# A decode layer with streamed K and V: the products of V are moved inside a loop trip, and the spreading of the heads is moved behind the loop

## The chip, the cores and the metric

The kernel runs on one core of a Trainium2 chip. The metric is the device time of one execution in microseconds (us). It was measured three times before the change: 297.23, 297.03 and 293.18 us, median 297.03 us. A profiled execution of the same program, from which all rows below come, took 297.05 us; the span of its instructions is 295.7 us.

## The reference

One decode step of a transformer layer for two sequences (B = 2, one new token each), in bf16:

```python
x  = A_x                                            # 2 x 1 x 640
q  = layernorm(x) @ wq                              # 32 heads of 192
k  = k_cache[:, :, 8192 - 2048:, :]                 # 2 x 32 x 2048 x 192, the last 2048 positions
v  = v_cache[:, :, 8192 - 2048:, :]
p  = softmax(q @ k.T * 192 ** -0.5)                 # per batch and head
h  = x + (p @ v, heads side by side) @ wo           # wo: 6144 x 640
h2 = h + (gelu(layernorm(h) @ w_gate) * (layernorm(h) @ w_up)) @ w_down   # 640 -> 1536 -> 640
```

K and V of the window are 50 MB each; the weights are some 22 MB. Each byte is read once and used for one or two vectors.

## The kernel before

**Tiles.** The window of a batch is cut into four quarters of 512 positions. One quarter of K, or of V, for all 32 heads is one transfer of 6144 KB into a 48 KB slot of each partition (`load_k`, `load_v`). A partition holds 128 positions of one head; 32 heads by four pieces make 128 partitions. A quarter is worked on as two groups of 64 positions per partition. So there are 16 groups g in all, 8 per batch; quarter g // 2 of K and of V belongs to group g.

**One group.** `transposes(g)` (line 560) turns the group's K on TensorE in 12 chunks of four matmuls, each chunk into one of four PSUM banks (`tps[0]` to `tps[3]`, used in turn); seven chunks are copied out to `ktr` by VectorE and five by ScalarE (lines 571 and 569). `scores(g)` (line 618) multiplies `ktr` with the masked queries into the bank `sps`. `softmax(g)` (lines 628 to 633) takes minimum and exponentials; `e_turn(g)` (line 657) and `e_blocks(g)` (line 661) put the exponentials, transposed, into the buffer `eblk[g % 2]`. `pv(g)` (line 673) multiplies them with V: 64 matmuls into the bank `ops` for even g and into `m1` for odd g.

**One trip.** TensorE and VectorE run a hardware loop of four trips J over groups 4J to 4J+3, that is two quarters, half a batch. After the trip's four groups `maxima`, `sums` and `combine` (lines 637 to 693) make the softmax's correction factors `wp` and `wfin`. The first quarter's products are copied from PSUM to `osb` (line 683). The second quarter's products, `pv(4J+2)` and `pv(4J+3)`, stand in `behind`, which runs at the start of the next trip (segment "pa", left out in trip 0) or behind the loop; `behind` also adds all four groups' products, weighted, into `osum` (lines 696 to 705).

**The heads.** After a batch, `heads_done(b)` scales `osum` into `onrm` and spreads it: four fp32 matmuls with the selection matrix `colsel` (line 714) into two PSUM banks, and for each bank a masked product, a reduction and a copy on VectorE (lines 720 to 724), which give `ot`, the stationary operand of the output projection. Batch 0's call stands in trip 2, in a segment of its own ("op", emitted under a condition on the trip); batch 1's stands behind the loop, ahead of the output projection `oproj` (line 738), the second layernorm and the feed-forward part (lines 806 to 889).

**What sets the order.** Each engine runs its instructions in the order in which the calls below are written; there is no planner. Between engines there are semaphores, derived from the reads and writes that each operation names. All large transfers are issued by SyncE in one fixed order: wq, k0, k1, v0, k2, v1, k3, v2, and so on to v7, then the four pieces of wo, w_gate, w_up and w_down. A transfer is issued when the last TensorE operation that reads the old content of its place is done (`done`, `pump`). The ring has three slots: two for K, one for V (v7 goes into a K slot). So v(i+1) is issued when `pv` of the odd group of quarter i is done, k(i+2) when the transposes of the odd group of quarter i are done, wo's first three pieces when `pv(13)` is done, wo's last piece, w_gate and w_up after `transposes(15)`, and w_down after `pv(15)`.

Of the kernel before, what the change touches and what calls it, by code (L numbers as in the profile page):

```python
# [6 lines left out]
F32 = mybir.dt.float32  # L7
# [5 lines left out]
B = 2  # L13
# [233 lines left out]
def bass_sequential_preLN__sliding_block_cached__geglu_ffn__decode_kernel(  # L247
# [12 lines left out]
    with ExitStack() as ctx:  # L260

        def sb(name, shape, dt):
            return ctx.enter_context(nc.sbuf_tensor(name, shape, dt))
# [64 lines left out]
        eblk = sb("eblk", [128, 2, 16, 4, 32], BF16)  # L328
        osb = sb("osb", [128, 2, DH], F32)
        osum = sb("osum", [128, DH], F32)  # L330
        onrm = sb("onrm", [128, DH], F32)
        cti = sm[:, 0:384].bitcast(I32).rearrange("p (k x) -> p k x", k=3)
        cxi = ktr[:, 0, :].bitcast(I32)[:, 0:512]
        cxf = ktr[:, 1, :].bitcast(F32)[:, 0:512]
# [80 lines left out]
        def dve(fn, R=(), W=(), X=(), cls=1):  # L415
            return P.op("dve", fn, R, W, X, cls=cls if looped else 0)
# [4 lines left out]
        def pe(fn, R=(), W=(), X=(), cls=0):  # L421
            return P.op("pe", fn, R, W, X, cls=cls)
# [4 lines left out]
        def ts(out, in0, s1, op0, s2=None, op1=None):  # L427
            def fn(e):
                kw_ = {"op1": op1} if op1 is not None else {}
                return e.tensor_scalar(out=out, in0=in0, scalar1=s1, scalar2=s2, op0=op0, **kw_)  # L430
            return fn
# [117 lines left out]
        def transposes(g, lo, hi):  # L549

            kk, ktoks = where["k", g // 2]
            kv = kk.bitcast(F32)
            for n in range(lo, hi):
                c, ch, scalar = TR[n]
                bank, x = tps[n % 4], ("t", n % 4)

                def fn(e, c=c, ch=ch, bank=bank):
                    for u in range(4):
                        off = 6144 * (g % 2) + 128 * (3 * (4 * ch + u) + c)
                        ins = e.transpose(bank[:, 128 * u:128 * (u + 1)], kv[:, off:off + 128], identf[:, :])  # L560
                    return ins

                pe(fn, R=ktoks + ["identf"], X=[x])
                if g % 2 == 1 and n == 11:
                    done(("k", g // 2))
                src = bank.bitcast(BF16)
                dst = ktr[:, c, 1024 * ch:1024 * (ch + 1)]
                if scalar:
                    act(lambda e, dst=dst, src=src: e.activation(out=dst, in_=src, func=ACT.Copy), W=[("kt", n)], X=[x])  # L569
                else:  # L570
                    dve(lambda e, dst=dst, src=src: e.tensor_copy(dst, src), W=[("kt", n)], X=[x], cls=0)  # L571
# [41 lines left out]
        def scores(g):  # L613
            def fn(e):
                for k in range(6):
                    for hg in range(4):
                        cols = ktr[:, k // 2, :].rearrange("p (a x w) -> p a x w", a=16, w=2)[:, :, 32 * hg:32 * (hg + 1), k % 2]
                        ins = e.matmul(sps[32 * hg:32 * (hg + 1), :], lhsT=rq[:, k, hg, :], rhs=cols, start=(k == 0),  # L618
                                       stop=(k == 5), tile_position=(0, 32 * hg))
                return ins  # L620

            pe(fn, R=[("rq", hg) for hg in range(4)] + [("kt", n) for n in range(12)], X=["s"])
            if g % 4 == 3 and g + 1 < 4 * NQ:
                q_masked((g + 1) // 8)

        def softmax(g):
            n = g % 4
            dve(lambda e: e.memset(gate[:, :], 0.0), W=["gate"], X=["s"], cls=0)
            dve(lambda e: e.tensor_tensor_reduce(  # L629
                out=sm[:, :].rearrange("p (u x) -> p u x", x=32), in0=sps[:, :].rearrange("p (u x) -> p u x", x=32),  # L630
                in1=mska[:, :].unsqueeze(1).to_broadcast([128, 16, 32]), scale=-1.0, scalar=2.0 * BIG, op0=ALU.add, op1=ALU.min,
                accum_out=nms[:, n:n + 1]), R=["mska"], W=["sm", ("nm", n)], X=["s"], cls=0)
            act(lambda e: e.activation(out=eexp[:, :], in_=sm[:, :], func=ACT.Exp, bias=nms[:, n:n + 1], scale=-1.0,  # L633
                                       accum_out=zr[:, n:n + 1]), R=[("nm", n), "sm", "gate"], W=["eexp", ("zr", n)])
# [24 lines left out]
        def e_blocks(g):  # L659
            for hg in range(4):  # L660
                dve(lambda e, hg=hg: e.tensor_copy(eblk[32 * hg:32 * (hg + 1), g % 2, :, hg, :],  # L661
                                                   et[32 * hg:32 * (hg + 1), :].rearrange("p (a x) -> p a x", x=32)),
                    R=["et"], W=[("eb", g % 2, hg)], cls=0)

        def pv(g):
            vv, vtoks = where["v", g // 2]
            bank, x = ((ops_, "o"), (m1, "m1"))[g % 2]

            def fn(e):
                for a in range(16):  # L670
                    for r in range(4):
                        t = 64 * (g % 2) + 4 * a + r
                        ins = e.matmul(bank[32 * r:32 * (r + 1), 0:DH],  # L673
                                       lhsT=eblk[:, g % 2, a, :, :].rearrange("p s x -> p (s x)")[:, r:128:4],
                                       rhs=vv[:, DH * t:DH * (t + 1)], start=(a == 0), stop=(a == 15),
                                       tile_position=(0, 32 * r), skip_group_check=True)
                return ins

            pe(fn, R=[("eb", g % 2)] + [("eb", g % 2, hg) for hg in range(4)] + vtoks, X=[x])
            if g % 2 == 1:  # L680
                done(("v", g // 2))
            if g % 4 < 2:
                dve(lambda e: e.tensor_copy(osb[:, g % 4, :], bank[:, 0:DH]), W=[("osb", g % 4)], X=[x], cls=0)  # L683

        def combine():
            def fn(e):
# [18 lines left out]
                    R=["wp", "osum"] + tok, W=["osum"], X=x, cls=0)  # L705

        def heads_done(b):
            dve(ts(onrm[:, :], osum[:, :], wfin[:, 0:1], ALU.mult), R=["wfin", "osum"], W=["onrm"])
            dve(lambda e: e.memset(nms[:, 4:5], BIG), W=[("nm", 4)])
            for y, (bank, x) in enumerate(((sps, "s"), (ops_, "o"))):  # L710
                def fn(e, y=y, bank=bank):
                    for j in range(2):
                        J = 2 * y + j
                        ins = e.matmul(bank[:, DH * j:DH * (j + 1)], lhsT=colsel[:, 128 * J:128 * (J + 1)], rhs=onrm[:, :],  # L714
                                       start=True, stop=True, skip_group_check=True)
                    return ins

                pe(fn, R=["colsel", "onrm"], X=[x])
            for y, (bank, x) in enumerate(((sps, "s"), (ops_, "o"))):
                dve(tt(sm[:, 0:384].rearrange("p (j a k) -> p j a k", j=2, k=12), bank[:, 0:384].rearrange("p (j a k) -> p j a k", j=2, k=12),  # L720
                       mask16[:, :].unsqueeze(1).unsqueeze(3).to_broadcast([128, 2, 16, 12]), ALU.mult), R=["mask16"], W=["sm"], X=[x])
                dve(lambda e: e.tensor_reduce(out=ot32[:, :], in_=sm[:, 0:384].rearrange("p (j a k) -> p j k a", j=2, k=12),  # L722
                                              axis=AX.X, op=ALU.add), R=["sm"], W=["ot32"])
                dve(lambda e, y=y: e.tensor_copy(ot[:, 2 * y:2 * y + 2, :, b], ot32[:, :].rearrange("p (j k) -> p j k", j=2)),
                    R=["ot32"], W=[("ot", y)])
# [47 lines left out]
        for J in range(4):  # L773
            if J > 0:
                P.loop_seg("pa", J)
                behind(4 * J - 2)
            if J == 2:
                P.loop_seg("op", J)
                heads_done(0)
            P.loop_seg("a", J)  # L780
            for g in (4 * J, 4 * J + 2):
                if g % 4 == 2:
                    pv(g - 2)
                    pv(g - 1)
                transposes(g, 0, 12)
                scores(g)
                softmax(g)
                transposes(g + 1, 0, 12)
                scores(g + 1)
                e_turn(g)  # L790
                softmax(g + 1)
                if g % 4 == 2:
                    maxima()
                e_blocks(g)
                e_turn(g + 1)
                e_blocks(g + 1)
                if g % 4 == 2:
                    sums()
                    combine()
        P.loop_seg()  # L800
        behind(14)
        heads_done(1)
        for J in range(4):
            oproj(J)

# [97 lines left out]
        P.emit("act", nc.scalar, sems)  # L903
        order = [(0, None, ["pa"]), (1, 3, ["op"]), "a"]
        P.emit_loop("dve", nc.vector, sems, 4, order)
        P.emit_loop("pe", nc.tensor, sems, 4, order)


# [26 lines left out]
```

## Time and profile before

| | |
|---|---|
| median of three runs | 297.03 us |
| profiled execution | 297.05 us, its span 295.7 us |
| mean granted TensorE clock | 0.854 |
| moved from HBM | 122.29 MB, 414 GB/s over the span |
| busy: TensorE matmul / VectorE / ScalarE / DMA queue of SyncE | 63% / 50% / 32% / 96.2% |

How to read it: the page gives busy time by engine, a strip in which each digit is a fortieth of the span (the share in tenths), the chain of work that ended last, and groups of instructions. In rows of instructions the first two numbers are the start and the duration in us; the bracket at the end is the engine's idle time ahead of the row and what ended it. PE is TensorE, DVE VectorE, ACT ScalarE, SPq the queue of SyncE. In a table of windows the columns are the stretch, its length, TensorE's busy time and instruction count, the granted TensorE clock as a share of full speed, the DMA engines' mean busy share, and GB/s.

### The profile page before, as it was taken

The numbers are of one execution on the slowest core, as the hardware profiler recorded it, in microseconds if no ns is written. First come the engines' busy times: TensorE is split into PE (matmuls) and PEld (weight loads), VectorE is DVE, ScalarE is ACT, GpSimd is POOL, SyncE is SP. The second block draws the span as 40 slices with busy tenths as digits, with TensorE's granted clock in tenths as the row PEclk, the third lists the DMA queues.
The fourth block names the chain that finished last, engine by engine and source line by source line (L and its number), as shares of the span: only waits on it lengthen the run. The fifth ranks groups of instructions, "written<-read, shape, count | busy, mean of one in ns | idle before, by whom it ended". The sixth has DMA issues, their size and how long they took to land.

```text
span 295.7 us, 6236 instructions
## 1 busy us (share of the span) xinstructions
PE 187.8 (63%) x2557; PEld 154.5 (52%) x2557; DVE 149.1 (50%) x365; ACT 94.7 (32%) x128; POOL 23.3 (8%) x69
## 2 busy tenths in 40 slices
PE   2007288508882987098728693986398429856785
PEld 1005186308771975097528572965396329636543
DVE  5000046711677567326674866367756715675522
ACT  1001036400671166115610661266046403650001
POOL 8930200000002000000020000001000000000000
PEclk9999969955998799669977998799689957996975
DMA  8999999999999999999999999999999999999970
GB/s 319 475 430 425 421 421 427 421 425 454 445 448 432 432 425 427 425 432 425 432 425 432 425 445 452 452 425 432 425 425 432 432 425 432 401 430 422 416 287 0
DMA packets 4204, 122.46 MB, mean 414 GB/s; under 512 B 478, under 2 KB 608, under 8 KB 1248
## 3 DMA queue, kind: packets, MB, share of 16 engines
q1 hardware_dynamic: 4188, 122.29, 96.2%
q8 instruction: 8, 0.13, 0.2%
q14 instruction: 4, 0.03, 0.0%
q10 hardware_dynamic: 4, 0.00, 0.0%
HBM read 122.29 MB, written 0.00 MB: 414 GB/s over the span
## 4 chain that ended last, share of the span: by engine, by line
DMA 61%; PE 26%; DVE 6%; issue 5%; ACT 1%; SPq 0%; DVEq 0%
DMA ring<-in_A_v_cache_dram 54%; PE ops L673 7%; DMA ring<-in_A_wq_dram 7%; PE m L673 6%; PE tpp L560 5%; PE tpp L580 2%; DVE eblk L661 1%; PE m L738 1%; DVE et L657 1%; DVE ot L722 1%; PE sps L714 1%; PE sps L834 1%; ACT ktr L569 1%; PE m L883 1%; PE ops L834 1%
## 5 line engine op out<-in xcount | busy, mean ns | idle before, releaser
L569 ACT ACTIVATE ktr<-tpp 128x1024 bf16<-128x1024 bf16 x80 | 76.6, 1018 | 95.1 <-PE tpp L560 95.1
L560 PE MATMUL tpp<-identf,ring 128*128 128x128 f32 x768 | 93.3, 281 | 10.7 <-DMA ring<-in_A_k_cache_dram 6.8
L560 PEld LDWEIGHTS tpp<-identf,ring 128*128 128x128 f32 x768 | 85.4, 144 | 20.4 <-DMA ring<-in_A_k_cache_dram 7.0
L571 DVE COPY ktr<-tpp 128x1024 bf16<-128x1024 bf16 x112 | 76.6, 691 | 28.7 <-PE tpp L560 27.2
L673 PE MATMUL ops<-ring,eblk 128*32 128x192 bf16 x512 | 22.1, 364 | 32.2 <-DMA ring<-in_A_v_cache_dram 28.2
L673 PEld LDWEIGHTS ops<-ring,eblk 128*32 128x32 bf16 x512 | 19.1, 144 | 34.5 <-issue 28.8
L618 PE MATMUL sps<-ktr,rq 128*32 128x512 bf16 x384 | 25.2, 390 | 13.8 <-DVE ktr L571 13.8
L633 ACT ACTIVATE eexp<-sm,nms 128x512 bf16<-128x512 f32 x16 | 11.6, 722 | 41.1 <-DVE nms L629 41.1
L618 PEld LDWEIGHTS sps<-ktr,rq 128*32 128x32 bf16 x384 | 10.2, 94 | 24.1 <-ACT ktr L569 17.5
L434 POOL TENSOR_TENSOR rq<-qs,mask 128x192 bf16<-128x192 bf16 x16 | 8.1, 537 | 182.5 <-PE sps L618 170.0
L673 PE MATMUL m<-ring,eblk 128*32 128x192 bf16 x512 | 20.3, 341 | 0.0
L661 DVE COPY eblk<-et 32x512 bf16<-32x512 bf16 x64 | 18.8, 294 | 1.8
L629 DVE CUSTOM_DVE_ANT_1 sm<-sps,mska 128x512 f32<-128x512 f32 x16 | 11.0, 687 | 16.4 <-issue 16.3
L673 PEld LDWEIGHTS m<-ring,eblk 128*32 128x32 bf16 x512 | 19.1, 141 | 0.0
L683 DVE COPY osb<-ops 128x192 f32<-128x192 f32 x4 | 1.4, 358 | 26.5 <-PE ops L673 26.5
L580 PE MATMUL tpp<-ring,xnT 128*32 128x384 bf16 x80 | 4.7, 407 | 15.4 <-DMA ring<-in_A_wq_dram 15.4
L687 PE MATMUL m<-wz,rowperm 128*128 128x6 f32 x8 | 2.4, 369 | 15.7 <-DVE wz L434 15.7
L657 DVE STREAM_TRANSPOSE et<-eexp 128x512 bf16<-128x512 bf16 x16 | 11.3, 706 | 1.0
L580 PEld LDWEIGHTS tpp<-ring,xnT 128*32 128x32 bf16 x80 | 2.7, 119 | 17.1 <-issue 15.5
L603 DVE CAST qs<-ops 128x384 bf16<-128x384 f32 x1 | 0.6, 558 | 20.9 <-PE ops L598 20.9
L687 PEld LDWEIGHTS m<-wz,rowperm 128*128 128x128 f32 x8 | 2.0, 311 | 16.1 <-DVE wz L434 16.1
L587 ACT ACTIVATE qrow<-tpp 128x768 bf16<-128x768 f32 x1 | 0.8, 811 | 19.6 <-PE tpp L580 19.6
(144 smaller groups left out, 102.7 us busy)
## 6 DMA issues: line engine op xcount, KB each, us to landing
ring<-in_A_k_cache_dram SPq DMA_DIRECT2D x8, 6144.0 KB, 24.5
ring<-in_A_v_cache_dram SPq DMA_DIRECT2D x8, 6144.0 KB, 24.2
ring<-in_A_wq_dram SPq DMA_DIRECT2D x1, 7680.0 KB, 21.4
ring<-in_A_wo_dram SPq DMA_DIRECT2D x4, 1920.0 KB, 15.7
ring<-in_B_w_gate_dram SPq DMA_DIRECT2D x1, 1536.0 KB, 16.7
ring<-in_B_w_up_dram SPq DMA_DIRECT2D x1, 1536.0 KB, 20.1
ring<-in_B_w_down_dram SPq DMA_DIRECT2D x1, 960.0 KB, 10.5
ring<-in_B_w_down_dram SPq DMA_DIRECT2D x1, 480.0 KB, 11.3
```

The lines of the kernel that those rows point to most:

```text
L434: return lambda e: e.tensor_tensor(out=out, in0=a, in1=b, op=op)
L560: ins = e.transpose(bank[:, 128 * u:128 * (u + 1)], kv[:, off:off + 128], identf[:, :])
L569: act(lambda e, dst=dst, src=src: e.activation(out=dst, in_=src, func=ACT.Copy), W=[("kt", n)], X=[x])
L571: dve(lambda e, dst=dst, src=src: e.tensor_copy(dst, src), W=[("kt", n)], X=[x], cls=0)
L580: ins = e.matmul(tps[0][32 * r:32 * (r + 1), 0:384], lhsT=xnT[:, c, 32 * J:32 * (J + 1)], rhs=wq[:, c, 1536 * J + 384 * r:1536 * J + 384 * ...
L618: ins = e.matmul(sps[32 * hg:32 * (hg + 1), :], lhsT=rq[:, k, hg, :], rhs=cols, start=(k == 0), stop=(k == 5), tile_position=(0, 32 * hg))
L629: dve(lambda e: e.tensor_tensor_reduce(out=sm[:, :].rearrange("p (u x) -> p u x", x=32), in0=sps[:, :].rearrange("p (u x) -> p u x", x=32) ...
L633: act(lambda e: e.activation(out=eexp[:, :], in_=sm[:, :], func=ACT.Exp, bias=nms[:, n:n + 1], scale=-1.0, accum_out=zr[:, n:n + 1]), R=[( ...
L657: dve(lambda e: e.transpose(et[:, :], eexp[:, :]), R=["eexp"] + [("eb", 0, 3)] * (g % 2), W=["et"], cls=0)
L661: dve(lambda e, hg=hg: e.tensor_copy(eblk[32 * hg:32 * (hg + 1), g % 2, :, hg, :], et[32 * hg:32 * (hg + 1), :].rearrange("p (a x) -> p a ...
L673: ins = e.matmul(bank[32 * r:32 * (r + 1), 0:DH], lhsT=eblk[:, g % 2, a, :, :].rearrange("p s x -> p (s x)")[:, r:128:4], rhs=vv[:, DH * t ...
L834: ins = e.matmul(bank[32 * r:32 * r + 2, 0:384], lhsT=hnT[:, c, :], rhs=cols[:, :, 3 * (r % 2):3 * (r % 2) + 3], start=(c == 0), stop=(c = ...
```

## The change

Three edits, which go together.

1. In a trip's second half, `pv(4J)` and `pv(4J+1)` stood ahead of `transposes(4J+2)`. They now stand behind `scores(4J+2)` and ahead of `transposes(4J+3)`, between the trip's third and fourth group. (They are the products of the trip's first quarter; they stand between the two groups of its second.)
2. The copies of these products to `osb` become a function, `o_rows`, called behind `maxima`, ahead of `e_blocks` of the third group. Before they followed `pv` directly.
3. `heads_done` keeps only the scaling to `onrm`, which gets one plane per batch; the rest becomes `spread(b)`. Both spreads now stand behind the loop: batch 0's ahead of `behind(14)`, batch 1's behind `heads_done(1)`. The second of a spread's two PSUM banks is `tps[0]` in place of `ops`. TensorE's loop has no conditional segment "op" any more; VectorE's keeps one, with the scaling and one memset.

```diff
-        onrm = sb("onrm", [128, DH], F32)
+        onrm = sb("onrm", [128, B, DH], F32)
...
-            if g % 4 < 2:
-                dve(lambda e: e.tensor_copy(osb[:, g % 4, :], bank[:, 0:DH]), W=[("osb", g % 4)], X=[x], cls=0)
+        def o_rows(g):
+            bank, x = ((ops_, "o"), (m1, "m1"))[g % 2]
+            dve(lambda e: e.tensor_copy(osb[:, g % 4, :], bank[:, 0:DH]), W=[("osb", g % 4)], X=[x], cls=0)
...
         def heads_done(b):
-            dve(ts(onrm[:, :], osum[:, :], wfin[:, 0:1], ALU.mult), R=["wfin", "osum"], W=["onrm"])
-            dve(lambda e: e.memset(nms[:, 4:5], BIG), W=[("nm", 4)])
-            for y, (bank, x) in enumerate(((sps, "s"), (ops_, "o"))):
+            dve(ts(onrm[:, b, :], osum[:, :], wfin[:, 0:1], ALU.mult), R=["wfin", "osum"], W=[("onrm", b)])
+
+        def spread(b):
+            for y, (bank, x) in enumerate(((sps, "s"), (tps[0], ("t", 0)))):
...
             if J == 2:
                 P.loop_seg("op", J)
                 heads_done(0)
+                dve(lambda e: e.memset(nms[:, 4:5], BIG), W=[("nm", 4)])
             P.loop_seg("a", J)
             for g in (4 * J, 4 * J + 2):
+                transposes(g, 0, 12)
+                scores(g)
+                softmax(g)
                 if g % 4 == 2:
                     pv(g - 2)
                     pv(g - 1)
-                transposes(g, 0, 12)
-                scores(g)
-                softmax(g)
                 transposes(g + 1, 0, 12)
                 scores(g + 1)
                 e_turn(g)
                 softmax(g + 1)
                 if g % 4 == 2:
                     maxima()
+                    o_rows(g - 2)
+                    o_rows(g - 1)
                 e_blocks(g)
...
         P.loop_seg()
+        spread(0)
         behind(14)
         heads_done(1)
+        spread(1)
         for J in range(4):
             oproj(J)
...
-        P.emit_loop("pe", nc.tensor, sems, 4, order)
+        P.emit_loop("pe", nc.tensor, sems, 4, order[:1] + order[2:])
```

More of the change, by code (lines that the diff above doesn't have):

```diff
@@ L713, in fn @@
                         J = 2 * y + j
-                        ins = e.matmul(bank[:, DH * j:DH * (j + 1)], lhsT=colsel[:, 128 * J:128 * (J + 1)], rhs=onrm[:, :],
+                        ins = e.matmul(bank[:, DH * j:DH * (j + 1)], lhsT=colsel[:, 128 * J:128 * (J + 1)], rhs=onrm[:, b, :],
                                        start=True, stop=True, skip_group_check=True)
                     return ins
-                pe(fn, R=["colsel", "onrm"], X=[x])
-            for y, (bank, x) in enumerate(((sps, "s"), (ops_, "o"))):
+                pe(fn, R=["colsel", ("onrm", b)], X=[x])
+            for y, (bank, x) in enumerate(((sps, "s"), (tps[0], ("t", 0)))):
                 dve(tt(sm[:, 0:384].rearrange("p (j a k) -> p j a k", j=2, k=12), bank[:, 0:384].rearrange("p (j a k) -> p j a k", j=2, k=12),
```

## The prediction

> **What bounds the kernel now.** I read the strips of the page first: is there a resource that is never idle, and where does it stop?
>
> ```profile
> span 295.7 us, 6236 instructions
> DMA  8999999999999999999999999999999999999970
> ```
>
> The DMA engines are full from the second slice to the 38th and empty in the last. So the kernel is a stream of bytes with a tail of compute behind it, and only two things can move the end: a gap torn into the stream, or a shorter tail. The chain of waits shows where the one hands over to the other (start, duration, what):
>
> ```profile
> 130.93 23.57 DMA ring<-in_A_v_cache_dram
> 217.42 24.28 DMA ring<-in_A_v_cache_dram
> 247.16 5.54 PE tpp L560 x48
> 269.83 2.69 PE ops L673 x64
> 293.62 0.33 DVE yrow L889
> ```
>
> Up to 241.7 us the chain runs through V's transfers: v3 lands at 130.93 + 23.57 = 154.5, v6 at 217.42 + 24.28 = 241.7. Six transfers lie between (k5, v4, k6, v5, k7, v6), so one takes 14.5 us, and k4 landed 14.5 ahead of v3, at 140.0. From 241.7 on compute ends last: `pv(12)`, `pv(13)`, two groups of transposes and scores, `pv(14)`, `pv(15)`, projection, feed-forward. Where the stream itself ends:
>
> ```profile
> 287.20:287.60 0.40, 0.20 (x5) 0.50 0.02 6
> L374 SPq DMA_DIRECT2D ring<-in_B_w_down_dram x4: 328/432/433, 274.9 to 276.2; - x4
> ring<-in_B_w_down_dram SPq DMA_DIRECT2D x1, 160.0 KB, 11.6
> ring<-in_B_w_up_dram SPq DMA_DIRECT2D x1, 1536.0 KB, 20.1
> ring<-in_B_w_gate_dram SPq DMA_DIRECT2D x1, 1536.0 KB, 16.7
> ```
>
> The last piece of w_down is issued at 276.2 and lands 11.6 us later, at 287.8; between 287.2 and 287.6 the DMA share is already 0.02. So compute ends some 5.8 us after the last byte, and that is nearly all that a shorter tail can win.
>
> **The change part by part: the last trip.** This is the trip whose order reaches the end.
>
> ```profile
> 236.39 1.23 DVE L661 COPY eblk<-et 32x512 bf16<-32x512 bf16 x4
> 241.84 2.76 PE L673 MATMUL ops<-ring,eblk 128*32 128x192 bf16 x64 [8.23 <-DMA ring<-in_A_v_cache_dram]
> 247.09 5.60 PE L560 MATMUL tpp<-identf,ring 128*128 128x128 f32 x48
> 253.55 1.60 PE L618 MATMUL sps<-ktr,rq 128*32 128x512 bf16 x24 [0.86 <-DVE ktr L571]
> 262.06 1.54 PE L618 MATMUL sps<-ktr,rq 128*32 128x512 bf16 x24 [0.86 <-DVE ktr L571]
> ```
>
> TensorE stands idle for 8.23 us ahead of `pv(12)` until v6 is there; k7, issued ahead of v6, landed earlier. Edit 1 puts `transposes(14)` and `scores(14)` into that idle time. They can't use all of it: VectorE works in order, and its copies of group 14 stand behind `e_blocks(13)`, which ends at 236.39 + 1.23 = 237.62. TensorE fills the four banks and then waits for VectorE. Trip 2 shows the same situation once, after the heads' work held VectorE up:
>
> ```profile
> 164.29 1.29 DVE L571 COPY ktr<-tpp 128x1024 bf16<-128x1024 bf16 x2
> 165.04 3.80 PE L560 MATMUL tpp<-identf,ring 128*128 128x128 f32 x32 [1.59 <-DVE ktr L571]
> 169.69 1.56 PE L618 MATMUL sps<-ktr,rq 128*32 128x512 bf16 x24 [0.86 <-DVE ktr L571]
> 171.18 2.40 PE L560 MATMUL tpp<-identf,ring 128*128 128x128 f32 x20
> ```
>
> From VectorE's first copy to the scores 169.69 - 164.29 = 5.40 us, to what follows on TensorE another 1.49. So `scores(14)` starts at about 237.65 + 5.40 = 243.05, and `pv(12)` at 244.54 instead of 241.84: it no longer waits for v6, but is 2.7 us later.
>
> Against that stands the clock. Duration times granted clock of two `pv` pairs and the clock between groups:
>
> ```profile
> 96.40:101.10 4.70, 4.70 (x129) 0.57 0.89 387
> 171.20:179.60 8.40, 7.30 (x74) 1.00 1.04 451
> 241.80:247.10 5.30, 5.26 (x129) 0.50 1.03 445
> ```
>
> 4.70 x 0.57 = 2.7 and 5.26 x 0.50 = 2.6: the pair costs about 2.7 us of full clock, and is slow because it follows idle time. Between groups the clock is 1.00, and in the new order the pair stands there. Bounds: 2.7 us at full clock, 5.26 at half. I take 2.8, since the row of 171.2 to 179.6 has the same work just ahead. `pv(13)` then ends at 247.34, practically where it ended before (247.1).
>
> From `transposes(15)`'s start to its scores goes 253.55 - 247.09 = 6.46 us (VectorE has nothing else there but group 14's softmax, which ends earlier): `scores(15)` at 253.8 instead of 262.06, a gain of 8.26 us.
>
> **The copies to `osb`** lay in idle VectorE time; now two of them stand between `maxima` and `e_blocks(14)`, with nothing to hide them:
>
> ```profile
> 244.65 0.36 DVE L683 COPY osb<-ops 128x192 f32<-128x192 f32 x1 [7.02 <-PE ops L673]
> ```
>
> 2 x 0.36 = 0.72 us lost; 7.54 us of gain remain when `combine` reaches TensorE.
>
> **The spread of batch 0** (edit 3), priced from that of batch 1:
>
> ```profile
> 275.82 0.92 PE L714 MATMUL sps<-onrm,colsel 128*128 128x192 f32 x4 [0.95 <-DVE nms L709]
> 276.58 0.81 PE L714 MATMUL ops<-onrm,colsel 128*128 128x192 f32 x4
> 276.78 0.56 DVE L434 TENSOR_TENSOR sm<-sps,mask 128x384 f32<-128x384 f32 x1 [1.00 <-PE sps L714]
> 277.37 0.81 DVE L722 TENSOR_REDUCE ot<-sm 128x24 f32<-128x384 f32 x1
> 278.22 0.18 DVE L724 CAST ot<-ot 128x24 bf16<-128x24 f32 x1
> ```
>
> Its four matmuls stand in TensorE's queue between `combine` and `pv(14)`, where nothing covers them. They occupy 275.82 to 277.39, 1.6 us; a following instruction can overlap their end, so I charge 1.4, with bounds of nothing (if the half clock of `pv(14)` ends sooner for the added activity) and 1.6. Neither bank has to be waited for: the readers of `sps` and `tps[0]` are done before `combine` starts.
> ```profile
> 269.76 2.76 PE L673 MATMUL ops<-ring,eblk 128*32 128x192 bf16 x64
> 274.92 1.75 SPq L374 DMA_DIRECT2D ring<-in_B_w_down_dram  x4
> 212.68 2.76 PE L673 MATMUL ops<-ring,eblk 128*32 128x192 bf16 x64 [0.34 <-DMA ring<-in_A_v_cache_dram]
> ```
>
> VectorE's six operations, 2 x (0.56 + 0.81 + 0.18) = 3.1 us, stand ahead of `behind`'s weighted sums, beside `pv(14)` and `pv(15)`, which last from 269.76 to w_down's issue at 274.92, 5.16 us; 2 us remain there for the sums that wait for no product. Without that cover they would cost 3.1. Taking the heads out of trip 2 wins nothing at the end: it frees these 3.1 us of VectorE ahead of 164.29, but that trip is paced by V, as TensorE waits for v5 at its end (third row).
>
> The other bank for the spread, the second plane of `onrm`, the moved memset and the branch gone from TensorE's loop I cost at nothing: same operations, same order on one engine, and no row shows the branch; within 0.2 us either way.
>
> **Sum of the compute.** 8.26 - 0.72 - 1.40 = 6.1 us of gain at the end of `pv(15)`, 268.8 instead of 274.92. With the tail unchanged, the final matmuls on w_down could start at 291.78 - 6.1 = 285.7 (third row).
>
> ```profile
> 284.40:288.20 3.80, 3.40 (x33) 0.55 0.50 190
> 288.20:293.60 5.40, 4.37 (x72) 0.50 0.00 0
> 291.78 1.78 PE L883 MATMUL m<-ring,uT 128*17 128x160 bf16 x48 [0.31 <-DVE uT L434]
> 261.60 0.43 SPq L374 DMA_DIRECT2D ring<-in_B_w_gate_dram  x1
> 262.07 0.91 SPq L374 DMA_DIRECT2D ring<-in_B_w_up_dram  x2
> ```
>
> **What is late next: the stream.** Earlier issues move no byte, since the queue holds enough work as it is: w_down is issued 6 us sooner but still follows w_up, and its last piece lands at 287.8 again. w_gate lands at 261.60 + 16.7 = 278.3 and w_up's large piece at 262.07 + 20.1 = 282.2, about when the earlier tail wants them (the stretches of the gate from 284.4 and of w_up from 288.2, less 6.1), so these cost at most half a microsecond, out of slack that the last piece takes anyway. The final matmuls therefore end with w_down: 287.8 plus its four matmuls (4 x 37 ns, from 1.78 us for 48) and some 0.2 us, 288.15 instead of 293.62 less the step to `yrow`. Gain 5.45 us; what follows (`yrow`, the output) is unchanged. Against the profiled execution: 297.05 - 5.45 = **291.6 us**; that execution lies 0.02 us above the median, so nothing is corrected.
>
> **The earlier trips** must leave the stream whole. Trip 1's last copy of `e_blocks(5)`:
>
> ```profile
> 120.23 1.23 DVE L661 COPY eblk<-et 32x512 bf16<-32x512 bf16 x4
> ```
>
> It ends at 121.46, so `pv(4)` starts at 121.5 + 5.40 + 1.49 = 128.4 and `pv(5)` ends at 131.2, after which v3 is issued; before it was 130.93. The DMA engines are busy with k4 until 140.0, nearly 9 us of cover. The issues of K come earlier by one `pv`.
>
> **The rivals.**
>
> *The pair stays slow.* If the clock is still 0.50 when `pv(12)` starts (TensorE does wait for VectorE inside group 14, by the row of trip 2 at 165.04 for 1.59 us), the pair takes 5.26, everything behind is 2.46 later, and the gain is 6.1 - 2.5 = 3.6: 293.4 us, compute still last. For it: each of the pairs before ran at 0.50 to 0.59. Against: in trip 2 the same wait left the clock at 1.00. The Trainium skill ("TensorE: Matmul & The Clock Gate", section "What's actually happening") has the gate fall after a whole idle window of about 3.4 us and open after a busy one, in windows that run freely. By that rule 1.59 us of waiting can't close it, and a pair behind a longer wait would start at half clock for a few microseconds, which agrees with the rows quoted.
>
> *The tail decides by its clock.* From 284.4 on TensorE ran at half clock, ahead of that at full clock, which is the projection:
>
> ```profile
> 278.50:284.40 5.90, 5.23 (x120) 1.00 1.00 405
> ```
>
> At full clock the feed-forward's 7.8 us of matmuls (3.40 + 4.37) would take half, 3.9 less, which is how far the fastest run before lies under the median (297.03 - 293.18 = 3.85). In the new order the last byte hides that. The other way, half clock in this stretch, would cost up to 5.2 us more, and half of it, the gate opening midway, 2.6: 6.1 - 2.6 = 3.5, 293.6 us.
>
> *The last byte comes sooner.* If w_down's end, where the DMA share falls off over 2.5 us, runs better with the requests queued sooner, or `pv(14)` warms up behind the spread, up to 7 us are won: 290.0 us, faster by over 2%.
>
> *V's slot comes free too late* (the other side, slower). If `pv(5)` ended behind k4's landing at 140.0, the stream would have a gap, in each of four trips. It decides from 9 us of delay against my 131.2; to be slower by 2% the gaps would have to add up to 5.9 + 5.45 = 11.4 us, about 3 us a trip, so `pv(5)` at 143: about 303 us. Only a wait that I don't see could do it; against it stands the cover just worked out.
>
> *It does not do what it says*: v6 is no longer waited for, but VectorE's order lets group 14 run no earlier. Then the spread and copies are pure loss, 2.1 us: 299.2. The stall of trip 2 speaks against it.
>
> **How the numbers follow.** Forecast 0.52 (290.7 to 292.6); slow pair 0.18 and slow tail 0.08 (292.6 to 295); last byte sooner 0.16 (289 to 290.7); slot too late 0.03; no effect 0.03. The range of 289.3 to 294.7 leaves out the last two and the edges of the others. 2%, about what a measurement of this kernel tells from no change, is 291.1 us: faster takes the last-byte case and a third of the forecast, 0.33; slower (over 303) 0.03; the rest, 0.64, is within 2%.
>
> **What the new profile would show.** `pv(12)` at about 244.5 with no wait for DMA and a clock near 1.00; `scores(15)` near 253.8; the two `osb` copies right ahead of `e_blocks(14)`; four L716 matmuls ahead of `pv(14)`; `pv(15)` ending near 268.8; the final matmuls waiting for w_down, with the last byte at 287 to 288 still, and the DMA strip without a gap. Wrong would be: a lower digit in the strip before slice 38, a wait of SyncE past 140 in trip 1, or final matmuls that wait for VectorE and not for DMA.

## The result and the profile after

The changed kernel takes 291.74 us (median of 19 runs, 291.57 to 293.39) against 296.22 us for the kernel before in the same sessions (19 runs, 292.65 to 297.23). The ratio is 0.989, 95% interval 0.986 to 0.992: faster by 1.1%, within 2%. The profiled execution took 291.70 us against 297.05.

The page of the changed kernel, the lines that answer to those of the kernel before:

```profile
span 290.4 us, 6202 instructions
DMA  8999999999999999999999999999999999999994
```

The DMA strip now runs full into the last slice. Compute no longer has a tail of its own behind the stream. The timeline of the last trip and of what follows it (start, duration, engine, line; the bracket is the idle time ahead):

```profile
238.53 3.80 PE L560 MATMUL tpp<-identf,ring 128*128 128x128 f32 x32 [2.89 <-DVE ktr L571]
243.19 1.61 PE L618 MATMUL sps<-ktr,rq 128*32 128x512 bf16 x24 [0.86 <-DVE ktr L571]
244.58 1.54 PE L673 MATMUL ops<-ring,eblk 128*32 128x192 bf16 x64
247.37 5.57 PE L560 MATMUL tpp<-identf,ring 128*128 128x128 f32 x48
253.80 1.56 PE L618 MATMUL sps<-ktr,rq 128*32 128x512 bf16 x24 [0.86 <-DVE ktr L571]
256.48 0.35 DVE L684 COPY osb<-ops 128x192 f32<-128x192 f32 x1
257.01 1.22 DVE L661 COPY eblk<-et 32x512 bf16<-32x512 bf16 x4
261.11 0.59 PE L688 MATMUL m<-wz,rowperm 128*128 128x6 f32 x2 [4.30 <-DVE wz L434]
261.98 1.63 PE L716 MATMUL sps<-onrm,colsel 128*128 128x192 f32 x4
263.40 1.49 PE L716 MATMUL tpp<-onrm,colsel 128*128 128x192 f32 x4
264.82 2.76 PE L673 MATMUL ops<-ring,eblk 128*32 128x192 bf16 x64
269.02 1.91 SPq L374 DMA_DIRECT2D ring<-in_B_w_down_dram  x4
282.25 1.36 PE L841 MATMUL ops<-ring,hnT 128*2 128x384 bf16 x20 [0.60 <-DMA ring<-in_B_w_up_dram]
285.66 1.66 PE L890 MATMUL m<-ring,uT 128*17 128x160 bf16 x36 [0.71 <-DMA ring<-in_B_w_down_dram]
287.50 0.72 PE L890 MATMUL m<-ring,uT 128*17 128x160 bf16 x12 [0.19 <-DMA ring<-in_B_w_down_dram]
288.28 0.33 DVE L896 CAST yrow<-m 113x160 bf16<-113x160 f32 x1 [3.07 <-PE m L890]
```

Group 14's scores come 10.4 us sooner (243.19, before 253.55), `pv(12)` waits for nothing, `scores(15)` comes at 253.80 instead of 262.06, and `pv(15)` ends at 269.02 instead of 274.92. Then the gain meets the stream: TensorE's final matmuls wait for w_down's pieces (0.71 and 0.19 us, after 0.60 us for w_up), and `yrow` is written at 288.28 instead of 293.62, 5.3 us sooner. Windows of the same execution (stretch, length, TensorE busy and count, granted clock, DMA share, GB/s):

```profile
244.50:247.40 2.90, 2.90 (x137) 1.00 1.18 508
264.80:269.00 4.20, 4.17 (x129) 0.67 1.00 424
287.20:287.60 0.40, 0.21 (x8) 0.50 0.07 26
```

The pair `pv(12)`, `pv(13)` ran at full clock, and the last byte arrives where it did before (DMA share 0.07 between 287.2 and 287.6, before 0.02). A window counts each packet whole where it starts, and in the trace a packet of K or V (48 KB) takes 1.8 us, so a share above 1 in a short window is no rate.

The profiles differ by 5.3 us, the medians by 4.5. This comes from the kernel before, whose executions don't all look like the profiled one (experiment 3).

### The profile page after: what moved, and what is told of

Read it like the earlier page. It is cut to its first block, busy times and chain, and to the rows that moved or that the text cites. A ratio compares the mean times of both kernels' runs of the same rounds, so it can differ in the third digit from the quotient of the medians.

```text
span 290.4 us, 6202 instructions
## 1 busy us (share of the span) xinstructions
PE 177.5 (61%) x2557; PEld 145.6 (50%) x2557; DVE 147.2 (51%) x364; ACT 94.8 (33%) x128; POOL 23.0 (8%) x69
## 4 chain that ended last, share of the span: by engine, by line
DMA 43%; PE 34%; issue 11%; DVE 9%; ACT 2%; SPq 1%; DVEq 0%
DMA ring<-in_A_v_cache_dram 24%; PE tpp L560 20%; DMA ring<-in_A_k_cache_dram 13%; DMA ring<-in_B_w_down_dram 6%; PE ops L673 6%; PE m L673 4%; DVE eblk L661 3%; DVE et L657 2%; PE sps L618 2%; DVE ktr L571 2%; ACT ktr L569 1%; ACT eexp L633 1%; PE sps L716 1%; SPq L374 0%; PE tpp L716 0%
## 5 line engine op out<-in xcount | busy, mean ns | idle before, releaser
L560 PE MATMUL tpp<-identf,ring 128*128 128x128 f32 x768 | 94.0, 282 | 19.6 <-DVE ktr L571 11.6
L560 PEld LDWEIGHTS tpp<-identf,ring 128*128 128x128 f32 x768 | 86.3, 144 | 28.6 <-DVE ktr L571 12.5
L673 PE MATMUL ops<-ring,eblk 128*32 128x192 bf16 x512 | 17.2, 305 | 23.7 <-DMA ring<-in_A_v_cache_dram 23.7
L673 PEld LDWEIGHTS ops<-ring,eblk 128*32 128x32 bf16 x512 | 15.2, 125 | 25.4 <-DMA ring<-in_A_v_cache_dram 24.4
L633 ACT ACTIVATE eexp<-sm,nms 128x512 bf16<-128x512 f32 x16 | 11.6, 723 | 41.2 <-DVE nms L629 41.2
L673 PE MATMUL m<-ring,eblk 128*32 128x192 bf16 x512 | 14.2, 267 | 2.8 <-issue 2.8
L704 DVE SCALAR_TENSOR_TENSOR osum<-ops,wp,osum 128x192 f32<-128x192 f32 x4 | 1.7, 418 | 25.8 <-PE ops L673 25.8
L673 PEld LDWEIGHTS m<-ring,eblk 128*32 128x32 bf16 x512 | 13.0, 116 | 3.0 <-issue 3.0
```

The costliest lines, as they stand in the source:

```text
L673: ins = e.matmul(bank[32 * r:32 * (r + 1), 0:DH], lhsT=eblk[:, g % 2, a, :, :].rearrange("p s x -> p (s x)")[:, r:128:4], rhs=vv[:, DH * t ...
```

## The experiments

Ten runs were made, one of them of the kernel before again. My theory: the stream of bytes sets the end of the changed kernel; the products' move brings the gain, the move of the heads costs a little where it can't be seen. Rivals: compute still ends last; the stream has less cover than the prediction gave it; the differences come from TensorE's clock.

**1 and 2. Each half of the change alone.** `pv_only` is the kernel before with edits 1 and 2:

```diff
+                transposes(g, 0, 12)
+                scores(g)
+                softmax(g)
                 if g % 4 == 2:
                     pv(g - 2)
                     pv(g - 1)
-                transposes(g, 0, 12)
-                scores(g)
-                softmax(g)
...
+                    o_rows(g - 2)
+                    o_rows(g - 1)
```

> Edits 1 and 2 alone: the products of V stand between the third and the fourth group, the heads of batch 0 stay in trip 2. If the end of the stream decides (w_down's last piece at 287.5 to 287.8), the time is that of the changed kernel, 291.7 us, though pv(14) starts some 2.8 us sooner for lack of the spread ahead of it; the final matmuls then wait longer for w_down. If compute still decides after the change, the time falls by the 1.8 us that the spread costs on TensorE, to about 290.

292.97 us (10 runs, 291.99 to 293.80), ratio to before 0.991 [0.987, 0.995]. Neither number came: it is slower than the changed kernel by 1.2 us, though it has no spread ahead of `pv(14)`. Its timeline and a window of it, and then the same of the changed kernel:

```profile
184.00 5.38 PE L560 MATMUL tpp<-identf,ring 128*128 128x128 f32 x32 [2.90 <-DVE ktr L571]
194.48 0.54 SPq L374 DMA_DIRECT2D ring<-in_A_v_cache_dram  x1
214.21 2.76 PE L673 MATMUL ops<-ring,eblk 128*32 128x192 bf16 x64 [4.78 <-DMA ring<-in_A_v_cache_dram]
196.00:203.00 7.00, 5.53 (x60) 1.00 0.91 358
```

```profile
180.35 3.79 PE L560 MATMUL tpp<-identf,ring 128*128 128x128 f32 x32 [2.90 <-DVE ktr L571]
189.24 0.54 SPq L374 DMA_DIRECT2D ring<-in_A_v_cache_dram  x1
212.89 2.76 PE L673 MATMUL ops<-ring,eblk 128*32 128x192 bf16 x64 [8.61 <-DMA ring<-in_A_v_cache_dram]
196.00:203.00 7.00, 1.33 (x21) 0.74 0.99 428
```

The heads of batch 0, left in trip 2, hold VectorE up at its start: the third group's transposes go on 3.65 us later (184.00 against 180.35). There they run partly at half clock and take 5.38 us instead of 3.79, another 1.6 us. So `pv(9)` ends later, v5 is issued at 194.5 instead of 189.2, `pv(10)` gets it 1.3 us later (214.21 against 212.89), and behind the issue the stream has a dent: 358 GB/s instead of 428 in the 7 us from 196, some 1.1 us of bytes. So moving the heads out of the loop is worth about 1.2 us once the products stand between the groups. I had it at nothing, and had tested it only against the order of the kernel before.

`spread_only` is the changed kernel with the products back ahead of the third group:

> Edit 3 alone: both spreads behind the loop, the products of V ahead of the third group as before. Compute decides here, so the spread of batch 0 ahead of pv(14) is paid: 1.4 to 1.8 us over the kernel before, about 298.5 us in its longer executions. If taking the heads out of trip 2 were worth anything (4 us of VectorE and TensorE), it would be no slower than before.

295.81 us (10 runs, 295.64 to 297.72), ratio to before 1.002 [0.998, 1.006]. The loss of 1.4 to 1.8 us did not show, so the expectation was wrong. But the kernel before spreads from 292.9 to 297.9 us in the same session and this one has no execution near 293, so the two medians compare unlike mixtures; the rows say more. From `combine` to the end of `pv(15)`, when w_down is issued, and the second half of the pair before:

```profile
244.53 1.71 PE L673 MATMUL m<-ring,eblk 128*32 128x192 bf16 x64
267.88 0.59 PE L687 MATMUL m<-wz,rowperm 128*128 128x6 f32 x2 [3.77 <-DVE wz L434]
268.75 1.63 PE L715 MATMUL sps<-onrm,colsel 128*128 128x192 f32 x4
271.59 1.80 PE L673 MATMUL ops<-ring,eblk 128*32 128x192 bf16 x64
273.22 1.49 PE L673 MATMUL m<-ring,eblk 128*32 128x192 bf16 x64
274.76 0.33 SPq L374 DMA_DIRECT2D ring<-in_B_w_down_dram  x1
```

The spread runs at half clock (1.63 us for matmuls that take 0.92 at full clock), but the clock is higher for the products behind it, which take 274.71 - 271.59 = 3.1 us instead of 5.16. In all 274.76 - 267.88 = 6.9 us, before 274.92 - 268.82 = 6.1: in this execution the spread costs 0.8 us net. The clock made that up elsewhere: `pv(13)` took 1.71 us instead of 2.81, and the final matmuls 1.01 us instead of 1.78. Whether edit 3 has a part in that, one profile doesn't show, so the price of the spread in this order stays open.

**3. The kernel before again.**

> The kernel before, unchanged, to see what its two groups of times are (about 293 and about 297 us). If the feed-forward's clock is the cause, the executions near 293 show a higher mean granted clock than those near 297 (0.854 in the profiled one), and a profile of a short one shows the stretch behind the projection at more than 0.50, with w_down landing near 287.5 as in the long ones. If the stream is the cause, w_down lands some 4 us sooner in a short one, at the same clock.

| granted clock of the execution | times of the 12 runs, us |
|---|---|
| 0.877 | 292.91, 292.98, 293.07, 293.18 |
| 0.859 | 295.63, 295.64, 295.84 |
| 0.853 to 0.855 | 296.07, 296.40, 296.77, 296.83, 297.20 |

The time follows the clock from group to group, though not inside the last one. None of the 0.877 executions is one whose rows are to be had, so where they gain was not seen. In the profiled one (0.853) the stretch behind the projection ran at half clock throughout:

```profile
284.40:288.20 3.80, 3.61 (x37) 0.50 0.50 191
288.20:293.00 4.80, 3.72 (x67) 0.50 0.00 0
```

At full clock these 7.3 us of matmuls would take half, 3.7 us less: about as far as the executions at 0.877 lie under those at 0.854. But the clock does not fit: with this stretch at 1.00 the mean of the profiled execution (0.853 over 295.1 us) would rise to about 0.866 only (an estimate from these two rows), so other stretches must differ too. And the profile of `before_short` (experiment 6, the same compute), one at 0.859, has this stretch at 0.50 throughout and gains ahead of it: `pv(15)` ends at 273.69 instead of 274.92. Where the executions at 0.877 gain stays open. The changed kernel's 19 runs lie at clocks from 0.856 to 0.883 without such an order (291.94 at 0.856, 292.09 at 0.882): its end waits for bytes, not for TensorE.

**4. w_down in other pieces.**

```diff
-WDC = ((0, 6), (6, 9), (9, 11), (11, 12))
+WDC = ((0, 6), (6, 10), (10, 12))
...
-WD_AT = (0, 7680, 7680 + 3840, 7680 + 3840 + 2560)
+WD_AT = (0, 7680, 7680 + 5120)
```

> The changed kernel with w_down in three pieces (6, 4, 2 blocks of 640) in place of four (6, 3, 2, 1), so that the last rows are 2560 bytes and not 1280. If the small rows are what lets the DMA share fall off over the last 2.5 us, the stream ends up to 0.8 us sooner and the time falls to about 291; if the fall-off is only the queue running dry, the last byte stays at 287.5 and four more matmuls stand behind it: 291.7 to 291.9 us.

291.75 us (4 runs, 291.66 to 292.62): the same as the changed kernel. The DMA share falls off in the same way (0.50 from 285.0 to 287.5, in the changed kernel 0.55), so the small rows are not the cause; what remains, that the queues of the 16 engines run dry at different times, was not shown.

**5 and 6. Fewer bytes.** The last three pieces of w_down are not loaded:

```diff
-            for i, (f0, f1) in enumerate(WDC):
+            for i, (f0, f1) in enumerate(WDC[:1]):
...
-            wd, wtoks = where["wd", i]
+            wd, wtoks = where["wd", 0]
```

> The changed kernel without the last three pieces of w_down (0.98 MB): the second six blocks of the final product use the first six blocks of w_down again, so the work of the engines is the same and part of the weights is left out. If the stream's end decides, it ends 2.3 us sooner (0.98 MB at 0.43 MB per us), and the final matmuls start when the engines are ready for them, at about 285.3 us, so they end 1.0 to 1.8 us sooner than 288.2: 290.0 to 290.7 us. If compute decides already, nothing changes: 291.7 us.

> The same omission in the kernel before: w_down's last three pieces are not loaded. Its compute ends 5.8 us behind the last byte in the longer executions, so nothing changes there (295.5 to 297 us); the short ones near 293 may fall a little, since their compute ends only some 2 us behind the last byte. If the stream decided before, all fall by 2 us.

`after_short`: 290.84 us (4 runs, 290.68 to 291.02), 0.9 us less than the changed kernel and a little more than the 290.0 to 290.7 expected. `before_short`: 296.16 us (10 runs, 295.44 to 297.33), ratio to before 1.006 [1.002, 1.010]: no gain; none of its executions lies near 293, so what was expected of the short ones was not tested. The final matmuls of `after_short`, and those of `before_short` with the issue of its w_down:

```profile
285.43 1.78 PE L890 MATMUL m<-ring,uT 128*17 128x160 bf16 x48 [0.73 <-DMA ring<-in_B_w_down_dram]
287.25 0.33 DVE L896 CAST yrow<-m 113x160 bf16<-113x160 f32 x1 [2.30 <-PE m L890]
```

```profile
273.69 0.33 SPq L374 DMA_DIRECT2D ring<-in_B_w_down_dram  x1
290.62 1.78 PE L883 MATMUL m<-ring,uT 128*17 128x160 bf16 x48 [0.31 <-DVE uT L434]
```

The same omission does what the theory says in each place: it shortens the kernel that waits for bytes (where the first piece is still waited for, 0.73 us), and does not shorten the one that waits for VectorE.

**7 and 8. Later compute.** The scaling of batch 1's heads is repeated three and ten times more (`range(4)` as shown, and `range(11)`):

```diff
-        heads_done(1)
+        for _ in range(4):
+            heads_done(1)
```

> The changed kernel with the scaling of batch 1's heads repeated three times more behind pv(15), each about 0.35 us on VectorE with TensorE waiting: compute is 1.1 us later. The final matmuls wait for w_down in sum about 1 us, so if the stream decides most of it is swallowed: 291.7 to 292.1 us. If compute decides: 292.8 us.

> As the one before, with ten repetitions, 3.5 to 3.8 us. If the stream decides, the first 1 to 1.2 us are swallowed and the rest is paid: 294.0 to 294.4 us. If compute decides: 295.3 us.

`after_late1`: 292.37 us (10 runs). Seven lie between 291.53 and 292.49, about as expected; three lie at 294.6, with clocks of 0.848 to 0.859 instead of 0.871 to 0.889. `after_late3`: 297.82 us (10 runs, 296.69 to 299.53), 6.1 us more than the changed kernel, for 3.5 us of added work: a miss. The profile of `after_late1` is one of its long executions; its projection and that of `after_late3`:

```profile
273.71 5.96 PE L740 MATMUL m<-ring,ot 128*2 128x320 bf16 x96
```

```profile
272.83 1.65 PE L716 MATMUL sps<-onrm,colsel 128*128 128x192 f32 x4 [5.19 <-DVE onrm L430]
276.55 6.05 PE L740 MATMUL m<-ring,ot 128*2 128x320 bf16 x96
```

The projection takes 3.43 us at full clock in the changed kernel. Here TensorE had waited ahead of the spread of batch 1 (5.19 us in the second kernel), and over the projection the clock was 0.57 and 0.56. So the slack of about 1 us is there and swallows a small delay, but a delay also brings the slow tail that the prediction held as a rival, and the projection alone then takes 2.5 us more. In `after_late3` the spread in front of it is slow too: 276.55 - 272.83 = 3.7 us, in the changed kernel 2.9. These 2.6 and 0.9 us are what the expectation lacked.

**9 and 10. How late v5 may be issued.** Batch 0's scaling is repeated in trip 2, eleven and twenty-two times more (`range(12)` as shown, and `range(23)`):

```diff
-                heads_done(0)
+                for _ in range(12):
+                    heads_done(0)
```

> The changed kernel with batch 0's scaling repeated eleven times more at the start of trip 2, 3.9 us of VectorE ahead of the copies of group 8. It delays pv(8), pv(9) and so the issue of v5 by 3.9 us, from 189.2 to 193.1, and nothing else that the end sees; k6 lands at about 198. If a transfer must only be issued ahead of the landing of the one before it, nothing changes: 291.7 us. If, as the run with the heads left in trip 2 suggests (v5 issued at 194.5, its landing 1.7 us late), it needs some 5 us of lead, v5 lands 0.4 us late: 292.1 us.

> The same with twenty-two repetitions, 7.8 us: v5 is issued at about 197.0, 1 us ahead of k6's landing. If only the landing counts, still 291.7 us. If some 5 us of lead are needed, v5 lands 4 to 4.5 us late and the whole stream behind it too: 295.7 to 296.2 us.

`after_v5_4`: 293.63 us (10 runs, 292.87 to 294.59), 1.9 more than the changed kernel. `after_v5_8`: 298.23 us (4 runs, 297.16 to 299.14), 6.5 more, which is more than either expectation. Both theories were too kind, for two reasons that the rows show. First of `after_v5_4`, then of `after_v5_8`:

```profile
164.90 5.38 PE L560 MATMUL tpp<-identf,ring 128*128 128x128 f32 x32 [3.50 <-DVE ktr L571]
185.87 5.38 PE L560 MATMUL tpp<-identf,ring 128*128 128x128 f32 x32 [2.89 <-DVE ktr L571]
196.39 0.53 SPq L374 DMA_DIRECT2D ring<-in_A_v_cache_dram  x1
195.00:198.00 3.00, 3.00 (x82) 1.00 0.80 279
```

```profile
181.75 0.54 SPq L374 DMA_DIRECT2D ring<-in_A_k_cache_dram  x1
188.98 6.67 PE L560 MATMUL tpp<-identf,ring 128*128 128x128 f32 x32 [2.90 <-DVE ktr L571]
200.80 0.53 SPq L374 DMA_DIRECT2D ring<-in_A_v_cache_dram  x1
198.00:202.00 4.00, 4.00 (x144) 1.00 0.00 0
202.00:202.25 0.25, 0.25 (x5) 1.00 6.03 1966
```

The delay does not stay 3.9 or 7.8 us. Behind a wait of TensorE for VectorE the clock falls, and the transposes there take 5.38 us (twice in `after_v5_4`) and 6.67 us where they take 3.80 at full clock; v5 is issued 7.2 and 11.6 us late.

And bytes are lost before the issue reaches the landing of k6. That landing lies one transfer ahead of v5's. In the changed kernel the chain of waits has v5 landing at 189.24 + 23.61 = 212.85, so k6 at about 198.3, and in `pv_only` and `after_v5_4` the stream is whole until shortly before. With 9.1 us between v5's issue and that landing, as in the changed kernel, nothing is lost; with some 3.8 (`pv_only`) the run is 1.2 us longer; with 1.9 (`after_v5_4`) it is 1.9. (The expectation has v5 in `pv_only` 1.7 us late; by the rows of experiment 1 it is 1.3.) The same trace has a lead that costs nothing: k6 of `after_v5_4` is issued at 178.66, some 5.1 us ahead of v4's landing by the same count, and from 175 to 189 the windows show 442 GB/s. So the loss begins at a lead between 3.8 and 5.1 us. By that, the 3.65 us that the heads take in `pv_only` would have lost no bytes without the 1.6 us that the fall of the clock added (a lead of 5.4 us); no run shows that by itself.

In `after_v5_8` k6 is itself issued late (181.75), and no packet starts between 198 and 202. There one part of the lead can be read: with the engines idle, the first packets start 1.2 to 1.45 us behind v5's issue at 200.80. The rest would be that the 16 engines finish k6 one after the other; that was not followed engine by engine.

## Why the prediction was right, point by point

The forecast was 291.6 us; measured were 291.74, and the sign and place of the gain were as forecast. Since the last byte sets the end, an error of some tenths in the compute terms below could not show in the time.

- **Group 14 into the wait for v6: right.** `scores(14)` was forecast at 243.05 and came at 243.19, `pv(12)` at 244.54 and came at 244.58. The stall of trip 2 was the right row to price it by, except for TensorE's wait inside the group: 2.89 us (the row at 238.53), where that stall had 1.59.
- **The pair at full clock: right, with luck.** 2.8 us forecast, 247.37 - 244.58 = 2.79 measured, clock 1.00. The rival of the slow pair was set aside on a wait of 1.59 us; the wait was 2.89. It did not occur here, but its mechanism is real: in trip 2 of `pv_only` the same 2.9 us of waiting was followed by a fall of the clock, as these windows of that kernel show.

```profile
181.10:183.90 2.80, 0.00 (x1) 1.00 0.98 421
184.50:185.00 0.50, 0.50 (x7) 1.00 2.50 1081
185.00:185.50 0.50, 0.50 (x5) 0.59 0.68 295
188.50:189.00 0.50, 0.50 (x6) 0.99 0.68 295
```

  The clock falls 1 us after TensorE has gone back to work (184.00) and rises 3.5 us later. The Trainium skill ("TensorE: Matmul & The Clock Gate", section "What's actually happening") has the gate judge by windows of about 3.4 us that run freely. The 3.5 us between fall and rise agree with its window; that 2.9 us without a matmul are enough does not agree with its whole idle window of 3.4, and the measurement decides: the reserve that the prediction read from that rule was thinner than it seemed.
- **The copies to `osb`: a little less.** 0.72 us forecast; `e_blocks` starts 0.53 us after the first copy (256.48 to 257.01), since the two overlap.
- **The tail: shorter than taken.** The prediction left it unchanged and let the final matmuls start at 285.7. Their operand `uT` was ready at 284.98 + 0.22 = 285.2, although `pv(15)` ended 0.2 us later than forecast and TensorE waited 0.60 us for w_up, where the prediction allowed half a microsecond. Parts of the feed-forward ran at full clock this time (1.36 us for the 20 matmuls at 282.25, 1.77 before). The last byte hid all of it.
- **The spread of batch 0: the term was mis-sized.** Forecast 1.4 us. From `combine` to `pv(14)` it is now 264.82 - 261.11 = 3.71 us, before 269.76 - 268.82 = 0.94, so the spread takes 2.8 us. I had priced it from a row at full clock, and it runs at half (1.63 us where the row had 0.92). The products behind it are faster in turn, 4.20 us instead of 5.16, as one of the bounds had it. The net price of 1.8 us lies outside the bounds of nothing to 1.6, and `pv(15)` ends at 269.02 instead of 268.8.
- **The stream as the floor: right,** and shown by both sides of experiments 5 and 6 and by the small delay of 7. The last byte was forecast at 287.8 and the final matmuls' end at 288.15; `yrow` followed at 288.28. Two small errors cancel in that: the last wait for w_down ended at 287.50, and 12 matmuls (0.72 us) stood behind it, not the four that were charged.
- **The earlier trips: right.** `pv(5)` was forecast to end at 131.2, and v3 was issued at 131.27.
- **"Taking the heads out of trip 2 wins nothing": wrong in the new order.** The sum missed it because the sum was made for the whole change, in which the heads are out. Experiment 1 gives 1.2 us, through the issue of v5 and not through the end of the trip, where the prediction had looked.
- **The cover of the stream: wrong in size.** I gave v3's issue nearly 9 us and let the rival of V's slot decide from 9 us of delay. By experiments 9 and 10, 3.9 us of delay on VectorE already costs 1.9 us. The rival did not come about, since the issues stayed where they were (v5 at 189.24, before 189.07), but it was much nearer than its 3 chances in 100 say.
- **The size against the median: off by what I left out.** 5.45 us were forecast from one execution, 5.3 came between the two profiles, 4.5 between the medians. The prediction saw that the fastest run of before lay 3.85 us below the median, and that the last byte would hide such a difference; it did not draw the conclusion that the measured gain is then an average over executions of before at 293 and at 297.

## What to carry to other kernels

Where a stream of transfers is never idle, a reordering can win only the compute behind the last byte, and its worth is read from two rows: the last landing and the end. An operation moved to where an engine has been waiting is priced at the clock of that place, not of the row it comes from. Before a step is called free because a transfer is in flight, ask how long ahead of the previous landing the next one is issued: here 3.8 us were too few and 5.1 enough, and a delay on one engine came out longer on the next.

## What the hardware showed that I had not expected

The clock of TensorE turned a delay into a larger one: 3.9 us on VectorE became 7.2 us at v5's issue.

A wait of 2.9 us could close the clock or not, and the records of the granted clock say on what it hung. In each trace the clock changes only at multiples of 3.41 us from one another (in the changed kernel 158.38, 199.34, 216.41, 260.78, 267.61, 284.68). In `pv_only` the stretch of 3.41 us that ends with the fall at 185.09 holds 2.3 us of the wait; in the changed kernel the boundaries cut the same waits in two, with at most 1.64 us in one stretch, and the clock stays. So whether a wait of this length closes the clock is a matter of where it falls.

And in trip 0 alone, TensorE stops within the 64 matmuls of `pv(1)` in the changed kernel:

```profile
73.09 0.51 PE L673 MATMUL m<-ring,eblk 128*32 128x192 bf16 x6 [2.80 <-issue]
```

It waits 2.8 us for nothing that the page names, and v1 is issued later by it (73.63, before 72.80). In `pv_only` the same place shows 3.6 us; the later trips show none. It cost nothing here, as the stream had its lead. One candidate stands in the trace: the instruction queue (q8 of the page, 8 packets of 16 KB in the whole execution) moves one of its packets in this stop, from 70.7 to 71.8, and in `pv_only` too, from 72.4 to 73.4, ending each time some 1.3 us ahead of the next matmul. That TensorE waits for these instructions fits, but no run shows it.
